# Weights loaded last, and every other wo load cut into 102 and 26 rows, in a one-query attention decode kernel

## Chip, cores and metric

One core of one Trainium2 chip. The time is that of the device, in microseconds (us), as a median of several executions of one program. "Before" took 1963.5 us (1963.5 to 1964.8). The record numbers two chips: e1 to e4 ran on one ("before" 1964.3 there), e5 to e10 on the other (1964.3 and 1964.0), so runs of both are compared to about 0.3 us.

## The reference, cut to what matters

```python
# x: 1 x 1 x 640; 32 heads; caches of 32768 keys of 192 numbers a head, bf16
def A(x, k_cache, v_cache, wq, wo):
    q = (x @ wq) per head
    p = softmax(q . k_cache * 192 ** -0.5)
    return (p . v_cache, heads joined: 6144 numbers) @ wo     # wo: 6144 x 640
def B(x, w1, w2):
    return relu(x @ w1) @ w2                                  # 640 x 1536 x 640
h = x + A(layernorm(x), ...)
out = h + B(layernorm(h), w1, w2)
```

K and V are 403 MB each, each byte used once. Everything else is small: wq and wo are 7.9 MB each, w1 and w2 2.0 MB each.

## The kernel before, where the change and the argument touch it

K and V come in loads of 3 MB, 64 keys for each of the 128 partitions, in three buffers each. The very last of them is cut into three of 40, 16 and 8 keys, so that little work is left behind the last byte. All loads are issued by one queue in the program's order.

```python
    def load_wo(pr):                       # once for two heads, 16 times
        t = wop.tile([P, 3, D], bf16, name="wo")
        nc.sync.dma_start(out=t[:], in_=wo_view[:, 3 * pr:3 * pr + 3, :])
        wo_t[pr] = t
    # ... cut ...
        for g in range(G):                 # chunks of keys
            h, c, ld, c0, jc, jp = chunks[g]
            end = ld - (len(loads) - NEND)           # NEND = 3: the short loads
            if end == 0 and c0 == 0:
                load_w("w1", B_w1, kpool, "kt", [(0, P)])      # takes a K buffer
                load_w("w2", B_w2, vpool, "vt", [(0, P)])      # takes a V buffer
                for i in range(NEND):
                    load_k(ld + i)
                for i in range(NEND):
                    load_v(ld + i)
            elif end < 0 and c0 == 0 and g > 0:
                load_k(ld)
                load_v(ld)
            if c == 1 and h % 2 == 0:
                load_wo(h // 2)
            if c == 3 and h % QG == QG - 2 and h + 2 < H:
                load_wq(h // QG + 1)
            transposes(g)                  # K by TensorE, for part of the scores
            if g > 0:
                pv(g - 1)
            scores_pe(g)
            # ... cut: the other scores on VectorE, softmax sums, projection ...
```

The softmax here doesn't subtract the row's maximum and nothing guards it: scores larger than these inputs give would overflow.

## Time and profile before

| | before |
|---|---|
| time | 1963.5 us |
| bytes loaded | 825 MB, 420 GB/s over the span |
| TensorE busy | 81% |
| chain that ended last | 78% K loads in flight |
| end | the 40-key K load lands at 1933.6, the span ends at 1962.3 |

The page gives busy shares by engine, the same in 40 slices of 49 us with GB/s, and the chain of work that ended last. These lines stand in the prediction below. Beside the views, the trace holds a landing record for each load and DMA engine, and the duration of each DMA packet; where the text speaks of landings or packets, it is these. (The loads with fewer than sixteen landings have one more record, which comes ahead of the others: the 5-row x load has 6 records; it is left out here.)

Two lines of work matter. All K and V pass at 430 GB/s, and what is left over at the end is the last chunks, the projection and the two small layers. And the sixteen DMA engines do not finish alike: in the last wo load, issued at 1798.8, six land by 1810.0 and eight at 1828.4 to 1830.1, some 20 us behind.

### The profile page before, as it was taken

How to read it: one execution, taken by the hardware profiler on the slowest of the kernel's cores; microseconds unless marked ns; L12 is line 12 of the kernel's file. 1: busy time of each engine (PE TensorE's matmuls, PEld its weight loads, DVE VectorE, ACT ScalarE, POOL GpSimd, SP SyncE). 2: the span in 40 equal slices, each digit the busy share in tenths (PEclk: the TensorE clock that was granted, in tenths of full speed). 3: DMA queues.
4: the chain of work that ended last, by engine and by line, in shares of the span. 5: the costliest groups of instructions: out<-in, count | busy, mean ns of one | idle time of the engine just before them, and what ended most of it. 6: DMA issues, size and time to landing. Idle time of an engine off the chain costs nothing.

```text
span 1962.3 us, 44905 instructions
## 1 busy us (share of the span) xinstructions
PE 1588.3 (81%) x20392; PEld 1116.2 (57%) x20392; DVE 1338.0 (68%) x654; ACT 1067.8 (54%) x2223; POOL 0.7 (0%) x6
## 2 busy tenths in 40 slices
PE   5887888888878788887888788887887878787876
PEld 4555555555556556565555555555555555555554
DVE  5766776667666676776777666766766767677664
ACT  4555555555555555555555555555555545555553
POOL 0000000000000000000000000000000000000000
PEclk9988899989998998988998988988989889999997
DMA  9999999999999999999999999999999999999994
GB/s 405 430 430 431 430 427 430 429 431 430 431 430 428 431 429 430 431 428 431 430 431 430 428 431 428 432 430 423 430 428 429 427 423 430 430 430 426 430 398 187
DMA packets 51506, 827.85 MB, mean 422 GB/s; under 512 B 4596, under 2 KB 17396, under 8 KB 18548
## 3 DMA queue, kind: packets, MB, share of 16 engines
q1 hardware_dynamic: 51316, 824.99, 98.5%
q8 instruction: 159, 2.61, 0.5%
q14 instruction: 31, 0.25, 0.0%
HBM read 824.97 MB, written 0.00 MB: 420 GB/s over the span
## 4 chain that ended last, share of the span: by engine, by line
DMA 78%; PE 16%; ACT 4%; DVE 2%; issue 1%; SPq 0%; ACTq 0%
DMA kt<-in_A_k_cache_dram 78%; PE o_ps L292 7%; PE tp L238 6%; ACT kT L239 3%; DVE pr L265 1%; PE sp L248 1%; PE sp L252 1%; PE sp L250 1%; ACT pB L255 0%; PE qps L204 0%; ACT pA L275 0%; DVE o_pair L313 0%; ACT row_e L207 0%; PE den L298 0%; PE attT L336 0%
## 5 line engine op out<-in xcount | busy, mean ns | idle before, releaser
L239 ACT COPY kT<-tp 128x1024 bf16<-128x1024 bf16 (+1 forms) x1025 | 905.2, 966 | 356.2 <-PE tp L238 353.2
L265 DVE TENSOR_TENSOR pr<-kt,qb 128x2304 f32<-128x2304 bf16 (+1 forms) x258 | 655.0, 2539 | 490.7 <-DMA kt<-in_A_k_cache_dram 487.2
L238 PE MATMUL tp<-ident_b,kt 128*128 128x128 bf16 x7677 | 593.1, 241 | 359.2 <-DMA kt<-in_A_k_cache_dram 283.8
L238 PEld LDWEIGHTS <-kt 128*128 128x128 bf16 x7677 | 524.8, 109 | 398.0 <-DMA kt<-in_A_k_cache_dram 294.6
L268 DVE TENSOR_REDUCE sc<-pr 128x12 f32<-128x2304 f32 (+1 forms) x258 | 654.3, 2536 | 27.6 <-ACT kT L239 1.4
L292 PE MATMUL o_ps<-vt,pB 128*2 128x384 bf16 x2559 | 498.6, 345 | 2.6 <-DMA vt<-in_A_v_cache_dram 2.6
L292 PEld LDWEIGHTS <-pB 128*2 128x2 bf16 x2559 | 203.6, 87 | 226.5 <-issue 65.0
L255 ACT ACTIVATE pB<-sp 128x20 bf16<-128x20 f32 (+1 forms) x258 | 48.5, 188 | 489.2 <-PE sp L252 489.2
L292 PE MATMUL o_ps<-vt,pA 128*2 128x384 bf16 x1537 | 291.9, 326 | 0.0
L248 PEld LDWEIGHTS <-kT 128*128 128x128 bf16 x2559 | 196.0, 96 | 85.8 <-issue 84.4
L248 PE MATMUL sp<-qm,kT 128*128 128x2 bf16 x2559 | 218.5, 164 | 0.5 <-ACT kT L239 0.5
L250 PE MATMUL sp<-qm,kT 128*128 128x1 bf16 x2559 | 214.9, 163 | 0.0
L252 PE MATMUL sp<-qm,kT 128*128 128x1 bf16 x2559 | 214.9, 163 | 0.0
L250 PEld LDWEIGHTS <-kT 128*128 128x128 bf16 x2559 | 198.6, 96 | 0.0
L292 PEld LDWEIGHTS <-pA 128*2 128x2 bf16 x1537 | 129.2, 84 | 120.9 <-issue 0.4
L252 PEld LDWEIGHTS <-kT 128*128 128x128 bf16 x2559 | 197.4, 96 | 0.0
L275 ACT ACTIVATE pA<-sc 128x12 bf16<-128x12 f32 (+1 forms) x258 | 52.9, 205 | 0.0
L255 ACT ACTIVATION_READ_ACCUMULATOR pB<-sp 128x1 f32 x258 | 50.2, 195 | 0.0
L275 ACT ACTIVATION_READ_ACCUMULATOR pA<-sc 128x1 f32 x258 | 49.4, 191 | 0.0
L304 DVE TENSOR_REDUCE rec<-den 128x1 f32<-128x20 f32 x32 | 5.7, 179 | 62.7 <-PE den L298 62.7
L314 ACT ACTIVATE o_pair<-o_ps,rec 2x192 f32<-2x192 f32 x32 | 13.2, 412 | 26.9 <-DVE o_pair L313 26.9
L326 PE MATMUL oT_ps<-ident_f,o_pair 2*128 2x1 f32 x192 | 24.2, 247 | 0.1
(60 smaller groups left out, 192.0 us busy)
## 6 DMA issues: line engine op xcount, KB each, us to landing
kt<-in_A_k_cache_dram SPq DMA_DIRECT2D x127, 3072.0 KB, 35.7
vt<-in_A_v_cache_dram SPq DMA_DIRECT2D x127, 3072.0 KB, 31.4
wq<-in_A_wq_dram SPq DMA_DIRECT2D x8, 960.0 KB, 34.7
wo<-in_A_wo_dram SPq DMA_DIRECT2D x16, 480.0 KB, 31.5
kt<-in_B_w_dram SPq DMA_DIRECT2D x1, 1920.0 KB
vt<-in_B_w_dram SPq DMA_DIRECT2D x1, 1920.0 KB
kt<-in_A_k_cache_dram SPq DMA_DIRECT2D x1, 1920.0 KB, 28.6
vt<-in_A_v_cache_dram SPq DMA_DIRECT2D x1, 1920.0 KB, 17.6
```

Source lines behind the costliest of these rows:

```text
L238: nc.tensor.transpose(out=tp[:, b, :], in_=kt[:, off:off + P], identity=ident_b[:])
L239: nc.scalar.copy(out=kT[:, b0:b0 + nb, :], in_=tp[:, 0:nb, :])
L248: nc.tensor.matmul(sp[:, 2 * i:2 * i + 2], lhsT=kT[:, 3 * i + 1, :], rhs=qm[:, 1:3], start=True, stop=False, skip_group_check=True)
L250: nc.tensor.matmul(sp[:, 2 * i:2 * i + 1], lhsT=kT[:, 3 * i, :], rhs=qm[:, 0:1], start=False, stop=False, skip_group_check=True)
L252: nc.tensor.matmul(sp[:, 2 * i + 1:2 * i + 2], lhsT=kT[:, 3 * i + 2, :], rhs=qm[:, 3:4], start=False, stop=True, skip_group_check=True)
L255: nc.scalar.activation(out=pB[:, 0:JP], in_=sp[:, 0:JP], func=F.Exp, scale=SCALE, accum_out=dsums[:, h, 2 * c + 1:2 * c + 2])
L265: nc.vector.tensor_tensor(out=pr[:, 0:JD, :], in0=kt[:, c0 * Dh:(c0 + JD) * Dh].rearrange("p (j d) -> p j d", d=Dh), in1=qb[:].unsqueeze(1 ...
L268: nc.vector.reduce_sum(out=sc[:, 0:JD], in_=pr[:, 0:JD, :], axis=mybir.AxisListType.X)
L275: nc.scalar.activation(out=pA[:, 0:JD], in_=sc[:, 0:JD], func=F.Exp, scale=SCALE, accum_out=dsums[:, h, 2 * c:2 * c + 1])
L292: nc.tensor.matmul(o[:], lhsT=p, rhs=vt[:, (c0 + j) * Dh:(c0 + j + 2) * Dh], start=first, stop=last)
L314: nc.scalar.activation(out=dst[:, 1, n0:n0 + Dh], in_=o[:, Dh:2 * Dh], func=F.Copy, scale=s[0:2, 1:2])
L326: nc.tensor.matmul(ps[:, b:b + 1], lhsT=src[:, i, b * P:(b + 1) * P], rhs=ident_f[0:2, i:i + 1], start=(i == 0), stop=(i == 1))
```

## The change: intent and diff

Intent, as far as the code tells it: let w1 and w2, which are used last, arrive last, behind the last V; and take some bytes from the engines that trail by giving more rows of wo to six of the sixteen.

```diff
     def load_wo(pr):
         t = wop.tile([P, 3, D], bf16, name="wo")
-        nc.sync.dma_start(out=t[:], in_=wo_view[:, 3 * pr:3 * pr + 3, :])
+        if pr % 2 == 0:
+            nc.sync.dma_start(out=t[:], in_=wo_view[:, 3 * pr:3 * pr + 3, :])
+        else:
+            nc.sync.dma_start(out=t[0:102], in_=wo_view[0:102, 3 * pr:3 * pr + 3, :])
+            nc.sync.dma_start(out=t[102:P], in_=wo_view[102:P, 3 * pr:3 * pr + 3, :])
 ... cut: load_w takes a number of pieces (chunks of the weight) instead of rows ...
             if end == 0 and c0 == 0:
-                load_w("w1", B_w1, kpool, "kt", [(0, P)])
-                load_w("w2", B_w2, vpool, "vt", [(0, P)])
                 for i in range(NEND):
                     load_k(ld + i)
                 for i in range(NEND):
                     load_v(ld + i)
+                load_w("w1", B_w1, kpool, "kt", 1)
+                load_w("w2", B_w2, vpool, "vt", 2)
 ... 
-        for n in range(DT):
-            for f in range(FT):
+        for f in range(FT):                # so that the first piece of w2 is used first
+            for n in range(DT):
 ... cut: the start and stop flags of the matmul, to match the new order ...
```

More of the change, by code (lines that the diff above doesn't have):

```diff
@@ L132, with load_w @@
     w_t = {}
-    def load_w(name, src, pool, tag, rows):
+    def load_w(name, src, pool, tag, pieces):
         n, N = src.shape[0] // P, src.shape[1]
-        assert n * N <= JL * Dh
+        assert n * N <= JL * Dh and n % pieces == 0
         t = pool.tile([P, JL * Dh], bf16, tag=tag, name=tag)
         v = t[:, 0:n * N].rearrange("p (c n) -> p c n", n=N)
-        for r0, r1 in rows:
-            nc.sync.dma_start(out=v[r0:r1], in_=src.rearrange("(c p) n -> p c n", p=P)[r0:r1])
+        for i in range(pieces):
+            c0, c1 = i * n // pieces, (i + 1) * n // pieces
+            nc.sync.dma_start(out=v[:, c0:c1], in_=src.rearrange("(c p) n -> p c n", p=P)[:, c0:c1])
         for c in range(n):
@@ L398 @@
         yps = ops.tile([P, DT], f32, tag="o_ps", name="yps")
-        for n in range(DT):
-            for f in range(FT):
+        for f in range(FT):
+            for n in range(DT):
                 nc.tensor.matmul(yps[:, n:n + 1], lhsT=w_t["w2", f][:, n * P:(n + 1) * P], rhs=h1T[:, f:f + 1],
-                                 start=(f == 0), stop=(f == FT - 1))
+                                 start=(f == 0 and n == 0), stop=(f == FT - 1 and n == DT - 1),
+                                 skip_group_check=True)
         y_col = small.tile([P, DT], f32, tag="y_col", name="y_col")
```

## The prediction

> **What bounds the kernel now.** I read the page's busy shares and 40 slices first, then the DMA queues and the chain that ended last, then the timeline of the end on the DMA queue's issuer and on TensorE.
>
> ```profile
> PE 1588.3 (81%) x20392; PEld 1116.2 (57%) x20392; DVE 1338.0 (68%) x654; ACT 1067.8 (54%) x2223; POOL 0.7 (0%) x6
> ...
> DMA  9999999999999999999999999999999999999994
> GB/s 405 430 430 431 430 427 430 429 431 430 431 430 428 431 429 430 431 428 431 430 431 430 428 431 428 432 430 423 430 428 429 427 423 430 430 430 426 430 398 187
> ...
> q1 hardware_dynamic: 51316, 824.99, 98.5%
> q8 instruction: 159, 2.61, 0.5%
> ...
> DMA 78%; PE 16%; ACT 4%; DVE 2%; issue 1%; SPq 0%; ACTq 0%
> ```
>
> No compute engine is full; the DMA engines are busy in every slice and move 423 to 432 GB/s in nearly all of them. 78% of the chain is K loads in flight. Only the last two slices (49 us each) fall off: 398 and 187. At 430, the missing (32 + 243) GB/s times 49 us is 31 us of transfer. That bounds what better packing of the end can give: under 1.6% of 1963.5.
>
> The timeline of the end, first the issuer's lines, then TensorE's (start us, us, engine, line, operation):
>
> ```profile
> 1893.83 0.38 SPq L140 DMA_DIRECT2D kt<-in_B_w_dram  x1
> 1902.00 0.38 SPq L140 DMA_DIRECT2D vt<-in_B_w_dram  x1
> 1904.96 18.24 SPq L123 DMA_DIRECT2D kt<-in_A_k_cache_dram  x3
> 1923.25 17.53 SPq L123 DMA_DIRECT2D vt<-in_A_v_cache_dram  x3
> ```
>
> ```profile
> 1933.61 2.10 PE L238 MATMUL tp<-ident_b,kt 128*128 128x128 bf16 x18 [9.45 <-DMA kt<-in_A_k_cache_dram]
> 1935.64 3.32 PE L292 MATMUL o_ps<-vt,pB 128*2 128x384 bf16 x10
> 1938.80 1.14 PE L292 MATMUL o_ps<-vt,pA 128*2 128x384 bf16 x6
> 1940.33 1.17 PE L238 MATMUL tp<-ident_b,kt 128*128 128x128 bf16 x18
> 1941.43 1.14 PE L292 MATMUL o_ps<-vt,pB 128*2 128x384 bf16 x6
> ...
> 1955.61 1.74 PE L394 MATMUL h1ps<-xn_ln,kt 128*128 128x1 bf16 x60 [1.36 <-DVE xn_ln L186]
> 1957.62 1.74 PE L401 MATMUL yps<-h1T,vt 128*128 128x1 bf16 x60 [0.27 <-ACT h1T L397]
> ```
>
> w1 and w2 are issued ahead of the last K and V, though w1 is first used at 1955.61. TensorE idles 9.45 us until the 40-row K load lands, and then runs nearly unbroken to the end. So the end is that landing (1933.57) plus 28.7 us.
>
> The landing records (one per DMA engine and load) tell more than the mean busy share. The first wo load lands on all its engines within 0.46 us. The last one (issued 1798.8) lands on six engines between 1809.5 and 1810.0, on one at 1810.7, on one at 1813.7, and on eight between 1828.4 and 1830.1. So six engines are unburdened, two a little late, and eight run 19 to 21 us behind. Every wait needs all sixteen, so the slow eight set the pace. Their burden is queue q8: one 16384-byte packet every 12 us. Around 22.4 us such a packet puts that engine's next 24576-byte packet 1.41 us late (it ends at 24.74, where 23.32 was due). 159/8 = 20 packets an engine times 1.41 = 28 us; the spread shows only 20 because the fast six run dry now and then (K issues that take 11 to 13 us, after a wo and a wq, near 126, 368, 609, 851, 1091, 1333 and 1573).
>
> [...] Hence 102 rows: 6 engines with 17 rows each; 26 rows: 13 engines with 2. The trace agrees as far as it goes: the 5-row x load has 5 landings from engines, not 16. Which engines the records belong to it does not tell.
> [...]
>
> **The change, part by part.**
> *Weights last.* On the slow engines V of the last full load lands at 1919.15, then w1 (4.6 us) and w2 (5.3 us), then K. Without those two, K starts at 1919.15; its 8 rows of 15360 bytes an engine at 0.573 us give 1923.75, against 1933.57. TensorE has just finished the load before (its last scores end at 1924.0). With warm matmuls (18 transposes in 1.17 instead of 2.10, 16 PV in 2.93 instead of 4.46) it would reach the first PV of this load 5.4 us later, at 1929.4. But V now comes behind the K loads of 16 and 8 rows: 1923.75 + 1.85 + 0.95 + 4.6 = 1931.2. From that PV to the end it was 1962.3 - 1941.4 = 20.9 us, which gives 1952.1: **10.2 us saved**. The weights then land at 1931.2 + 1.85 + 0.95 + 4.7 = 1938.7 (w1; wanted at 1945.4) and about 1944 to 1945.4 (w2, with one more fetch; wanted at 1947.4). So both are hidden, by 6.7 and 2 us. Slots: w1 now waits for the last full K's use (VectorE ends it at 1922.1) and w2 for its PV (about 1928); both come while the slow engines still have V to load.
>
> *wo rows.* A wo row is 3 packets of 1280 bytes, 0.0523 us apart. Eight of the 16 wo loads change. Engines of the six carry 17 + 2 = 19 rows instead of 8: 11 x 3 x 0.0523 = 1.73 us more, 13.8 us in all. Engines 6 to 12 carry 2: 18 packets less, 0.94 us, 7.5 us in all; 13 to 15 none, 10.0 us less. If the fast six are 0 to 5 (six free ones and six chosen: I take this as the intent), the slow ones lose 7.5 us of their 28 and the fast take 13.8, still 28 - 7.5 - 13.8 = 6.7 us less than the slow: **7.5 us saved**.
>
> *Rest.* Eight more issues at 0.4 us on an issuer that mostly waits, w2 in two pieces, and 60 matmuls in another order (1.74 us again): nothing on the path.
>
> Sum: 1963.5 - 10.2 - 7.5 = 1945.8.
>
> **The rivals.**
> 1. [...] the slow ones gain nothing, and the 57 packets of a fast engine take up to twice as long: 57 x 0.0523 = 3 us more, which with the 1.73 is 4.7 us a load, 38 us in all, above the 28 that the slow ones trail by. The fast six would then be the last ones. [...] Against it: someone chose six engines and every other load, which looks tuned. Nothing gained gives 1953; the full loss gives 1965 to 1990.
> 2. *Wrong engines.* If some of the lowest six are among the slow ones, they get 13.8 us more: 1963.5 - 10.2 + 13.8 = 1967. The match of six to six speaks against it.
> 3. *A new wait at the end.* w2 now ends the loads with 2 us of slack, so a late slot[...] (the K issue at 1904.96 took 15.2 us behind w2) can cost 1 to 4 us: 1947 to 1950. The two pieces, and using the first piece first, cover 1 us of it.
> 4. *TensorE becomes the bound* in the last loads, where it has no pause left: at most the 1.8 us that V leaves, hence no change.
>
> **Range and chances.** Both parts as reckoned, or with 1 to 5 us lost: about 0.6, 1945 to 1951. wo gives nothing: 0.2, about 1953. wo harms: 0.2, 1958 to 1990. I put the prediction at **1948.0**, range **1943 to 1963**. Faster by 2% needs 1924, more than the 31 us of empty transfer allow with any tail left: 0.01. Slower by 2% needs 2003: 0.02. Within 2%: 0.97.
>
> **What would show it.** In the changed profile: TensorE's 9.45 us idle before the last 18-transpose group gone; that group near 1916 to 1924; the last two slices filled; no wait of h1ps or yps for a DMA. In the landings: spread of the late loads at 5 to 10 us instead of 20, the 102-row pieces with six landings. [...] The prediction is wrong if the last K lands later than 1924, or if w2 is what the end waits for.

The 17 and 2 rows an engine are the author's estimate, 102 rows shared evenly by six engines and 26 by thirteen. The landings of the change have those counts, six and thirteen in each cut load, and the latest of the two pieces are 0.31 to 0.35 us apart, about 6 packets of 0.0523 us, so it is very likely one engine with 2 rows more. That all six are among the thirteen was not shown. That packets take "up to twice as long" in rival 1 was the author's assumption. No record names its engine: the numbers 0 to 15 and "lowest" are the order told at e4. A "fetch" is a packet of q8.

## The result, and the profile after

The changed kernel took **1997.5 us** (1996.4 to 1999.7, four runs), against 1963.5. The ratio is 1.0173, 95% interval 1.0155 to 1.0191. A ratio here is the mean time of one kernel's runs over that of the other's in the same rounds, so it is not quite the ratio of the medians. That is 34 us slower, where 15.5 us faster was predicted with a range up to 1963. The class "within 2%" held; the direction and the size did not.

The page after, GB/s in the 40 slices (50 us each):

```profile
DMA  9999999999999999999999899999999999999996
GB/s 403 432 403 428 432 428 430 395 431 430 429 431 382 432 430 429 432 388 430 430 430 431 355 431 431 430 430 383 431 430 430 430 371 430 431 430 431 366 431 245
```

Before, the middle of this line was flat. Now there are eight dips (403, 395, 382, 388, 355, 383, 371, 366), one for each wo load that is cut. Together they miss 397 GB/s of 430, for a slice of 49.9 us: 46 us of transfer. The end is better than before (431 and 245 in place of 398 and 187).

The stretch view, first before, in a stretch in which a wo load lands (issued at 1074.8), and then after, around two of the cut loads (columns: stretch, its length, busy time and count of TensorE, its weight loads, VectorE, ScalarE, GpSimd, granted clock, DMA share, GB/s):

```profile
1084.00:1108.00 24.00, 18.47 (x236) 13.12 (x234) 16.02 (x10) 12.43 (x26) 0.00 (x0) 0.86 1.00 425
```

```profile
120.00:136.00 16.00, 11.41 (x147) 8.13 (x147) 10.39 (x5) 7.81 (x16) 0.00 (x0) 0.90 1.01 434
136.00:146.00 10.00, 8.91 (x97) 5.84 (x96) 6.68 (x7) 5.77 (x12) 0.00 (x0) 0.81 1.02 289
...
1108.00:1122.00 14.00, 9.79 (x134) 6.40 (x131) 9.08 (x4) 7.56 (x16) 0.00 (x0) 1.00 0.65 215
```

Before, a wo load does not show: 425 GB/s. After, in the first cut load (136 to 146) the DMA share is 1.02, so no engine idles, and yet they move 289 GB/s: the packets themselves take longer. In this stretch the mean 24576-byte packet takes 1.31 us instead of 0.91. In a later cut load (1108 to 1122) there are both slow packets and idle engines (share 0.65). The idle engines there have to do with the issuer: without its hold (e5, below) the share in such a stretch is 1.00. Its timeline around this wo load, before and after (start, duration, line, what it issued):

```profile
1074.46 0.33 SPq L123 DMA_DIRECT2D vt<-in_A_v_cache_dram  x1
1074.84 0.68 SPq L113 DMA_DIRECT2D wo<-in_A_wo_dram  x1
1078.01 0.33 SPq L123 DMA_DIRECT2D kt<-in_A_k_cache_dram  x1
```

```profile
1098.37 0.33 SPq L128 DMA_DIRECT2D vt<-in_A_v_cache_dram  x1
1098.75 0.33 SPq L117 DMA_DIRECT2D wo<-in_A_wo_dram  x1
1099.12 13.52 SPq L118 DMA_DIRECT2D wo<-in_A_wo_dram  x1
1112.76 7.64 SPq L128 DMA_DIRECT2D kt<-in_A_k_cache_dram  x1
```

The second piece holds the issuer for 13.5 us, and the next K is issued 13.6 us after that piece instead of 3.2 us after the wo load. That gives three suspects: the slow packets, the held issuer, and the wrong engines. The landings speak for the last: at the end of the run fifteen engines lie within 2.6 us, and one alone lands 13 us after the first. The pieces of 102 rows have six engine landings each, and the last of the six falls further behind the fifth from load to load (1 us in the first, 12 us in the load above, 16.5 us in the last).

The end, on TensorE:

```profile
1973.86 1.14 PE L298 MATMUL o_ps<-vt,pB 128*2 128x384 bf16 x6 [1.22 <-DMA vt<-in_A_v_cache_dram]
...
1987.82 1.74 PE L400 MATMUL h1ps<-xn_ln,kt 128*128 128x1 bf16 x60 [1.36 <-DVE xn_ln L192]
1989.82 1.74 PE L407 MATMUL yps<-h1T,vt 128*128 128x1 bf16 x60 [0.27 <-ACT h1T L403]
```

The idle of 9.45 us before the last K is gone, V is waited for by 1.2 us, and neither h1ps nor yps waits for a DMA. The weights part did what it should.

### The profile page after: what moved, and what is told of

Read it like the earlier page. It is cut to its first block, busy times and chain, and to the rows that moved or that the text cites. A ratio compares the mean times of both kernels' runs of the same rounds, so it can differ in the third digit from the quotient of the medians.

```text
span 1994.7 us, 44915 instructions
## 1 busy us (share of the span) xinstructions
PE 1601.5 (80%) x20392; PEld 1127.2 (57%) x20392; DVE 1338.0 (67%) x654; ACT 1067.3 (54%) x2223; POOL 0.7 (0%) x6
## 4 chain that ended last, share of the span: by engine, by line
DMA 77%; PE 16%; ACT 4%; DVE 1%; issue 1%; SPq 0%; ACTq 0%; DVEq 0%
DMA kt<-in_A_k_cache_dram 73%; PE o_ps L298 8%; PE tp L244 6%; DMA vt<-in_A_v_cache_dram 4%; ACT kT L245 3%; DVE pr L271 1%; PE sp L254 1%; PE sp L258 1%; PE sp L256 1%; PE qps L210 0%; ACT pB L261 0%; ACT pA L281 0%; SPq L128 0%; ACT row_e L213 0%; DVE o_pair L319 0%
## 5 line engine op out<-in xcount | busy, mean ns | idle before, releaser
L244 PE MATMUL tp<-ident_b,kt 128*128 128x128 bf16 x7677 | 603.3, 243 | 372.6 <-DMA kt<-in_A_k_cache_dram 298.8
L244 PEld LDWEIGHTS <-kt 128*128 128x128 bf16 x7677 | 534.9, 111 | 410.8 <-DMA kt<-in_A_k_cache_dram 309.2
L332 PE MATMUL oT_ps<-ident_f,o_pair 2*128 2x1 f32 x192 | 24.2, 247 | 0.1
```

The source lines that it names most:

```text
L244: nc.tensor.transpose(out=tp[:, b, :], in_=kt[:, off:off + P], identity=ident_b[:])
L332: nc.tensor.matmul(ps[:, b:b + 1], lhsT=src[:, i, b * P:(b + 1) * P], rhs=ident_f[0:2, i:i + 1], start=(i == 0), stop=(i == 1))
```

## The experiments

Theories. **P**: a wo load in pieces of fewer than 128 rows gets slower, and so do the K and V packets beside it. **R**: engine 5, one of the six, is one of the eight slow engines, and 11 more rows a load make it the last. **S**: the held issuer sends K and V late, and engines run dry. **B**: the weights part harms the end.

### Each part alone (e1, e2)

e1 keeps the weights part and undoes the wo part; e2 is the reverse.

```diff
# e1, against the change
-        if pr % 2 == 0: ... else: ... two pieces
+        nc.sync.dma_start(out=t[:], in_=wo_view[:, 3 * pr:3 * pr + 3, :])
```

> Only the weights-last part, every wo load in one piece. Theory A (the wo pieces cost all of the loss, the weights gain what was predicted): 1953 us, 10 us under before, TensorE's idle of 9.45 us before the last 18 transposes gone. Rival B (w2 as last load is what the end waits for, so the end itself lost time): 1963 us or more, with yps waiting for a DMA.

> Only the wo pieces, weights where they were before. Theory A: the 34 us of loss plus the 10 us that the weights gained, so 2005 to 2010 us. Rival B: about 1990 us, if the end is to blame for part of it.

Measured: e1 1954.6 us, ratio 0.9951 (0.9938 to 0.9963); e2 2005.7 us, ratio 1.0212 (1.0197 to 1.0228). So the weights gain 9.7 us, the wo part alone costs 41.4, and beside the weights part it costs 1997.5 - 1954.6 = 42.9. B is out. TensorE at the end of e1:

```profile
1925.15 1.17 PE L239 MATMUL tp<-ident_b,kt 128*128 128x128 bf16 x18
...
1931.42 1.14 PE L293 MATMUL o_ps<-vt,pB 128*2 128x384 bf16 x6 [0.85 <-DMA vt<-in_A_v_cache_dram]
...
1945.38 1.74 PE L395 MATMUL h1ps<-xn_ln,kt 128*128 128x1 bf16 x60 [1.36 <-DVE xn_ln L187]
1947.38 1.74 PE L402 MATMUL yps<-h1T,vt 128*128 128x1 bf16 x60 [0.27 <-ACT h1T L398]
```

No idle before the 18 transposes, and the PV that was said to start at 1931.2, held by V, starts at 1931.42, held by V.

### Which engines are slow (e4, one look)

```diff
+            if c == 2 and h >= 16:         # one tiny load a head, of 1, 2, ... 16 rows
+                i = h - 16
+                k = i + 1
+                nc.sync.dma_start(out=probe[i][0:k, :], in_=A_wo[0:k, 0:8])
```

> Before, plus sixteen tiny loads of 1, 2, ... 16 rows (heads 16 to 31)[...]: each one's landings show how far its engines trail. Prediction as made (the lowest six are the six free engines): the loads of 1 to 6 rows land within 1 us, and late landings (11 to 21 us) come only from 8 rows up. Theory A2 (a fetch-burdened engine is among the lowest six, as one 102-row piece's landings of the changed kernel suggest): one landing more than 10 us late already with 6 rows or fewer. Time about as before, 1963 to 1966.

These loads of k rows, k from 1 to 16, have k engine landings each. Each follows a V load in the queue, so its landings can be set against that V's first landing (us later):

```
rows  landings of the tiny load, us after the first landing of the V load before it
 4    0.2 0.4 4.4 7.5
 5    0.2 0.4 1.6 4.4 7.4
 6    0.2 0.4 1.6 4.4 8.0 18.6
 7    0.2 0.4 1.7 5.4 8.0 18.6 20.2
 8    0.2 0.3 0.4 0.4 4.0 7.3 18.8 18.8
 9    0.2 0.2 0.2 0.3 0.6 3.5 7.7 19.7 19.8
10    0.2 0.2 0.3 0.3 0.4 2.0 6.0 18.1 18.1 18.2
```

With the sixth and the seventh engine a landing some 19 us late is added; with the eighth and ninth an early one; with the tenth to the fifteenth (rows not all shown) a late one each; with the sixteenth an early one. That each load takes the engines of the one before and one more fits these landings; the trace names no engine, so it is taken, not shown. Numbered in this order from 0, the slow eight are 5, 6 and 9 to 14. The first six are not the six free ones: in the 6-row load they are three free ones (0.2, 0.4, 1.6), the two that trail a little (4.4, 8.0), and engine 5 (18.6). The 102-row pieces, with six landings of which one falls behind, fit these six. The look took 1964.0 us (one execution), about as before, so the probes cost nothing to speak of. In this order R stands: one of the six is slow; what it costs comes next.

### The same with engine 5 left out (e7)

```diff
-            nc.sync.dma_start(out=t[0:102], ...); nc.sync.dma_start(out=t[102:P], ...)
+            nc.sync.dma_start(out=t[0:95], ...);  nc.sync.dma_start(out=t[95:P], ...)
```

> As the change, but cut at row 95: [...] 5 engines with 19 rows and 11 engines with 3, so that engines 0 to 4 (none of the eight slow ones by the map) take the extra rows and engine 5 gets 3 rows instead of 19. Theory R alone (only the slow engine's rows count): 5 rows less for the slow engines, 0.157 us a row, 8 loads, 6 us under weights last: 1948. Theory P[...]: the gain on engine 5 is there (clearly under the change's 1997), [...] so 1970 to 1985.

Measured: 1980.1 us (1979.7 to 1987.5), ratio 1.0092 (1.0076 to 1.0109). Engine 5 has 16 rows less in eight loads (3 for 19, if pieces are shared evenly) and the time is 17.4 us less. Most of that was waiting. What the span has beyond all packets, summed and divided by 16 engines, is the mean idle time of an engine: 8.0 us in e1, 26.3 in the change, 11.7 here. It was not the issuer's hold that went:

```profile
L118 SPq DMA_DIRECT2D wo<-in_A_wo_dram x8: 459/16438/19247, 111.0 to 1821.7; - x8
```

All issues of more than 1.5 us last 279 us together here and 282 in the change (97 in e1). So the waiting goes with engine 5. The 17.4 us are no clean price for its rows, though, since another engine is now the last: the latest landings of the 95-row piece and of the 33-row piece are less than 1 us apart in every cut load, hence very likely of one engine that has rows of both, one of the first five. And with engine 5 relieved the kernel is still 25.5 us above e1, where R alone wanted 6 below. Most of the loss is not R.

### Pieces without any imbalance (e3, e9)

e3 cuts at row 64. Each piece lands on 16 engines, so each gets 4 + 4 rows if they are shared evenly, the 8 of a whole load. e9 is its control: also two pieces, but cut between columns, so that each piece has all 128 rows.

```diff
# e3
+            nc.sync.dma_start(out=t[0:64], in_=wo_view[0:64, 3 * pr:3 * pr + 3, :])
+            nc.sync.dma_start(out=t[64:P], in_=wo_view[64:P, 3 * pr:3 * pr + 3, :])
# e9
+            nc.sync.dma_start(out=t[:, 0:2], in_=wo_view[:, 3 * pr:3 * pr + 2, :])
+            nc.sync.dma_start(out=t[:, 2:3], in_=wo_view[:, 3 * pr + 2:3 * pr + 3, :])
```

> As the change, but the eight loads are cut at row 64: each of 16 engines gets 4 + 4 rows, so no engine has more or fewer packets than in one piece[...]. Theory P[...]: 1280-byte packets of about 0.1 us in these loads, K and V packets beside them stretched, and 1963 to 1985 us. Theory R (only the number of rows on the slowest engine counts[...]): 0.055 us packets and 1953 us, as weights last alone.

> The control for the halves: weights last, the eight loads in two pieces as well, but cut between the three 640-column blocks, so that each piece has 128 rows[...], 16 + 8 packets. Theory P[...]: no loss, 1954 to 1956, packets of 0.055 us. Rival (two pieces as such, one more issue and one more semaphore round, cost it): 1975 or more.

Measured: e3 1983.4 us, ratio 1.0099 (1.0086 to 1.0113), a loss of 28.8 us against e1 without one row more for anybody. e9 1954.5 us, ratio 0.9954 (0.9941 to 0.9966), e1's time. So two pieces cost nothing; pieces of fewer rows do. The issue lines of wo in e3, then in e9 (durations in ns, shortest/median/longest), and e3's stretches around one cut load:

```profile
L117 SPq DMA_DIRECT2D wo<-in_A_wo_dram x8: 607/610/722, 110.1 to 1824.2; - x8
L118 SPq DMA_DIRECT2D wo<-in_A_wo_dram x8: 601/604/604, 110.9 to 1824.8; - x8
```

```profile
L117 SPq DMA_DIRECT2D wo<-in_A_wo_dram x8: 428/430/453, 110.2 to 1799.6; - x8
L118 SPq DMA_DIRECT2D wo<-in_A_wo_dram x8: 459/464/491, 110.6 to 1800.1; - x8
```

```profile
1090.00:1100.00 10.00, 9.21 (x133) 6.70 (x130) 5.73 (x4) 7.53 (x19) 0.00 (x0) 1.00 1.00 433
1100.00:1106.00 6.00, 4.82 (x74) 3.47 (x72) 5.86 (x3) 4.37 (x9) 0.00 (x0) 1.00 1.00 326
```

The pieces themselves do not hold the issuer, all engines are busy, and 326 GB/s pass instead of 433. That is what P says, by itself: same rows, same number of landings, slow only where the pieces are cut by rows. Why is not shown: no record tells which engine moves which row. Nor do the cuts part writing from reading: a piece with other rows of the tile also has other rows of wo. e6 (below) speaks for the writing: there the rows of the tile come from other rows of wo than in e1, in whole loads, and nothing is lost (1954.6 us in both).

The packets tell where the time is. Summed and divided by 16 engines, the 24576-byte K and V packets take 1861.2 us in e1 and 1861.2 in e9, but 1884.1 in e3: 22.9 us more, though no K or V load was touched. The wo packets add 3.7. Together 26.6 of e3's 28.8 us. In the change it is 19.6 + 4.6 = 24.2 us, and the rest of its 42.9 is the waiting told above: 26.3 us idle instead of 8.0. In e3, where no engine has more rows, it is 9.8.

### The held issuer taken away (e5, with e6 as its partner)

wo's rows are regrouped so that a row of the tile is one packet of 3840 bytes instead of three of 1280; the transposition of the heads' outputs is turned to match, and the result stays right. e5 has the change's cut, e6 has whole loads.

```diff
-    wo_view = A_wo.rearrange("(b p) n -> p b n", p=P)
+    wo_view = A_wo.rearrange("(r p b) n -> p r b n", p=P, b=3)     # loads take wo_view[:, pr]
-            src = o_pair[pr % 2]                    # lhsT=src[:, i, b * P:(b + 1) * P]
+            src = o_pair[pr % 2][:].rearrange("q i (p b) -> q i b p", b=3)   # lhsT=src[:, i, b, :]
```

> The change with wo's rows regrouped (row p of the tile holds three neighbouring rows of wo, o_pair is turned to match), so that a wo row is one packet of 3840 bytes: same bytes, engines[...], a third of the packets. Theory S (the loss comes from the issuer, held 10 to 16 us by the second piece[...], so that later K and V loads come late): the hold and the loss go, within 5 us of e6. Theory P+R ([...] 11 more rows for a fetch-burdened engine): the hold goes but the loss stays, 35 to 45 us above e6.

> Weights last, wo in one piece, rows of 3840 bytes: the fair partner of e5. By all theories 1 to 2 us under weights last alone (8 rows save about 0.08 us a load, 16 loads): 1953 us.

The issue lines of the two pieces, in the change and in e5:

```profile
L117 SPq DMA_DIRECT2D wo<-in_A_wo_dram x8: 328/328/337, 111.2 to 1836.2; - x8
L118 SPq DMA_DIRECT2D wo<-in_A_wo_dram x8: 9802/13254/15582, 111.6 to 1836.6; - x8
```

```profile
L117 SPq DMA_DIRECT2D wo<-in_A_wo_dram x8: 325/330/709, 109.9 to 1841.3; - x8
L118 SPq DMA_DIRECT2D wo<-in_A_wo_dram x8: 316/319/328, 110.3 to 1841.7; - x8
```

And around one cut load of e5, for the 0.65 and 215 GB/s of the change:

```profile
1108.00:1124.00 16.00, 11.10 (x133) 6.92 (x131) 8.94 (x4) 7.42 (x16) 0.00 (x0) 0.82 1.00 329
```

The hold is gone (0.3 us instead of 13), and the loss is not: e5 took 2006.2 us, ratio 1.0214 (1.02 to 1.0228), which is 51.6 us above e6 with 1954.6, ratio 0.995 (0.9938 to 0.9963). The hold is therefore not needed for the loss, and S falls as its main cause: the engines idle for 26.4 us on average (10.3 in e6) without it, and for 11.7 with it in e7. That the loss became 9 us larger than with short packets was not expected. The K and V packets show it too: 29.9 us more an engine than in e6, against 19.6. Why long wo packets hinder the others more stays open. e6 was also expected 1.3 us under e1 and is level with it.

### The cost doubled (e10)

```diff
-        if pr % 2 == 0:
+        if pr < 0:          # never: all 16 wo loads in pieces of 102 and 26 rows
```

> The suspected cost doubled: all 16 wo loads in pieces of 102 and 26 rows, weights last. If each split load costs the same 5.4 us (43 us over eight): 1954.6 + 86 = 2040 us, and engine 5 with 22 instead of 11 rows a pair of loads stays alone at the end. If the first eight had mostly used up slack and further ones cost less (or moved the bound to another engine): under 2025.

Measured: 2034.2 us, ratio 1.0355 (1.0339 to 1.037): 79.6 us above e1, 5.0 a load against 5.4 with eight. Nearly proportional, so each cut load pays for itself; there was no slack that the first eight used up.

### A version that beats both (e8)

```diff
-                for i in range(NEND):
-                    load_k(ld + i)
-                for i in range(NEND):
-                    load_v(ld + i)
+                for i in range(NEND):
+                    load_k(ld + i)
+                    load_v(ld + i)
```

> e6 with the last three K and V loads in turn (K, V, K, V, K, V) instead of three K and then three V: the 0.85 us that TensorE waits for V in weights last goes, nothing else moves. 1 us under e6; if V was not what held the end, the same as e6.

Measured: 1952.5 us, ratio 0.994 (0.9928 to 0.9953), the fastest of all, 2.0 us under e6, which it changes in this alone. The PV of the 40-key load no longer waits for V:

```profile
1928.82 1.14 PE L293 MATMUL o_ps<-vt,pB 128*2 128x384 bf16 x6
```

e6's profile shows 1.40 us idle at this place:

```profile
1930.08 1.14 PE L293 MATMUL o_ps<-vt,pB 128*2 128x384 bf16 x6 [1.40 <-DMA vt<-in_A_v_cache_dram]
```

That is 1.40 of the 2.0 us, so most of the gain is the expected one.

| run | what it has | us | against e1 |
|---|---|---|---|
| before | | 1964.0 to 1964.3 | +9.6 |
| e1 | weights last | 1954.6 | |
| e9 | and two pieces by columns | 1954.5 | 0 |
| e7 | and 95 + 33 rows | 1980.1 | +25.5 |
| e3 | and 64 + 64 rows | 1983.4 | +28.8 |
| the change | and 102 + 26 rows | 1997.5 | +42.9 |
| e10 | 102 + 26 rows in all 16 | 2034.2 | +79.6 |
| e8 | weights last, K and V in turn, long wo rows | 1952.5 | -2.1 |

## Why the prediction was wrong, point by point

- *What bounds the kernel, and that eight engines trail because of q8's packets:* the eight trailing engines are right, e4's map finds them. The trace of before shows q8 behind it. The packet at 22.41 is followed by a 24576-byte packet of 1.41 us, where the others take 0.91. At the wo load issued at 111.1, ten packets of q8 had begun, and against the first five landings six engines trailed by 1.4 to 1.7 us and two by 3.0 to 3.1: 6 + 2 x 2 = 10 delays. At the one issued at 234.0 it was twenty, with four engines 2.8 to 3.0 us and four 4.3 to 4.5 us behind: 4 x 2 + 4 x 3 = 20. Over the whole run that gives 159/8 x 1.41 us = 28 us, an estimate; the trailing stays near 20 because five K and V loads issued from 1332.6 to 1798.4 take the first engines 7.8 to 9.5 us instead of 7.3. The page calls the queue's kind "instruction"; what it fetches was not shown, and no run took it away.
- *Weights last, 10.2 us saved:* right. e1 saved 9.7, by the steps named, with the last 40-key K at 1923.9 for 1923.75, the PV at 1931.42 for 1931.2, and V as what it waits for.
- *wo rows, 7.5 us saved:* this is the step that failed, and with it the sum: beside the weights part it cost 42.9 us. It rested on "If the fast six are 0 to 5 (six free ones and six chosen: I take this as the intent)". The trace could not tell which engine a landing belongs to, and the gap was filled with a guess about the author. By e4's order, engine 5 is one of the slow eight. Instead of losing 7.5 us of work it gained 11 rows a load, and the others wait for it: 14.1 us by the change over e3, 17.4 over e7, near what rival 2 had reckoned (13.8) without believing it.
- *Rival 1:* dismissed because "someone chose six engines and every other load, which looks tuned". The runs give a loss of its kind the larger part: 28.8 us in e3 with no engine given a row more; whether its mechanism is the reason was not shown. It was also mis-sized as it stood. It let the slow engines break even ("the slow ones gain nothing") and counted only the longer wo packets of the fast six. In fact the K and V packets got longer, by 19.6 us an engine on average, four times the 4.6 us of the wo packets. The wo packets did get longer: 1280 bytes took 0.089 us on average in the first cut load, against 0.055 around the same load before.
- *The rivals were taken one at a time.* The first was given 1965 to 1990, the wrong engines 1967. Both came: 1954.6 + 28.8 (e3, no engine with more rows) leaves 14.1 of the 1997.5 for engine 5. That the two simply add is taken, not shown.
- *The held issuer:* rival 3 looked for it at the end only. It came at each cut load, for 10 to 16 us. e5 says that it is not what the loss needs. In e7, with as much hold, the engines idle 3.7 us more than in e1, so in the change it can hardly be more than a few us; its exact share is not shown.
- *Range and chances:* "within 2%" held. The range 1943 to 1963 did not, since harm was given 0.2 in all and only part of it lay inside.

## What to carry to other kernels

When sixteen DMA engines finish unevenly, find out which they are before moving bytes between them: loads of 1, 2, 3 ... rows beside the main stream showed it here in one run, at no cost (1964.0 us, "before" 1964.3). Rows are not free to move: here eight wo loads cut by rows slowed the K and V packets beside them and cost 28.8 us (e3), and cut by columns nothing (e9), so beside a stream at 430 GB/s a load should first be tried with all its rows in one piece. A change with two parts is worth running in its parts: here one half was worth 9.7 us and was hidden behind the other's 43.
